# Four q/k buffers, eight first slots turned on TensorE, one assignment product per column set, and a new written-out order

## The chip, the cores and the metric

The kernel runs on one core of a Trainium2 chip. The core has a matrix engine (TensorE, "PE", whose weight loads are listed apart as "PEld"), VectorE ("DVE"), ScalarE ("ACT"), GpSimd ("POOL") and a sync engine ("SP") that issues nearly all transfers; 16 DMA engines carry them. Each engine works through its own list of instructions in order, and engines wait for each other by semaphores. The metric is the time of one execution on the device, in microseconds (us).

## The reference

Two layers follow each other. The first is attention inside clusters: queries and keys are each assigned to the nearest of 16 centroids, and a query attends only to keys of its own cluster. The second is a feed-forward network with a three-tap convolution along the sequence.

```python
# attention: q, k, v are [4, 8, 768, 64]; centroids [8, 16, 64]
q_assign = argmax(einsum(q_n, c_n)); k_assign = argmax(einsum(k_n, c_n))   # unit vectors
mask   = q_assign[:, :, :, None] == k_assign[:, :, None, :]
scores = where(mask, q @ k.T / 8, -1e9)
x      = softmax(scores) @ v                     # to [4, 768, 512]
# feed-forward: w_in [512, 1024], conv_w [3, 1024], w_out [1024, 512]
h    = relu(x @ w_in)
gate = sigmoid(conv3(h))
out  = (h * gate) @ w_out                        # float32 [4, 768, 512]
```

## The kernel before, in words

**Pairs and slots.** Two heads of one batch make a pair g, 16 in all (four per batch). A slot t is one pair against a part of its queries: 512 queries (the first part, `a` = 0) or 256 (`a` = 1). Of the eight slots of a batch the first four are its pairs with 512 queries, the next four the same pairs with 256. So slots 0 to 3 and 4 to 7 are batch 0, and 24 to 27 and 28 to 31 are batch 3. Scores are made with the keys on the partitions. One exponential step `E` works on 1024 columns; a slot has six of them in the first part and three in the second, 144 in all.

**The mask as extra rows.** The cluster of a query and of a key becomes three numbers (`BR`), which are appended to the 64 rows of q and k. The score product then has 67 rows and gives a large negative number wherever clusters differ, so that no mask step is needed.

**The way of a pair.** `LQ`, `LK` (pairs 0 to 7) or eight block loads `LZ` (pairs 8 to 15) bring q and k into a `qk_in` buffer, of which there are `NQK` in turn. `T` turns them on TensorE (line 295) and `Q` evicts the result, or `Z` turns blocks of 32 by 32 on VectorE (line 304). `A` multiplies them with the centroids (line 337), each of four 32-column sets of the array giving the similarities of a quarter of the tokens. `M0` to `M6` find the largest on VectorE; `M5` and `M6`, which pack the result, can be on GpSimd (`M5p`, `M6p`). `K` turns the pack on TensorE, `B` evicts it, and the transfer `BX` lays it as bias rows under q and k. `CC` casts q and k to half width, and the transfer `CX` shifts the second head to the lower partitions. `LV` loads v and `CV` casts it. In the first pair, one head at a time, `CD`, `KB` and `BB` do the work of `CC`, `K` and `B`.

**The way of a slot.** `S` is the score product, `E` the exponential on ScalarE (line 454), `V` the product with v (line 467), `P` the reciprocal of the row sums, `N` the normalization (line 490). The result has to be turned before it can enter the feed-forward part. There are two ways for it: `XD`, a transposing transfer on the sync engine's queue (line 508), or `X`, a transpose on TensorE (line 496), with `Ya` or `Yd`, an eviction on ScalarE or VectorE (line 308 or 310).

**The feed-forward part** goes in 24 units, six per batch: four units on the first 512 tokens, two on the other 256. `I` multiplies with w_in (line 534) and `R` evicts with the ReLU. `C` carries columns from one part to the next, on GpSimd. `a`, `b`, `c` are the taps on VectorE (lines 572 and 574), or `W` the taps on TensorE (line 580) with diagonal weights that `_tp` has made. `H` is the tanh on ScalarE, `G` the gate on VectorE (line 605), `O` the product with w_out (line 617, two of its eight terms a step), `F` its eviction into one of four `o_sb` buffers, `FX` the store. `LW` and `CW` load and cast the weights.

**What sets the order.** Nothing is scheduled at run time: `PLAN` is a list of some 1600 of these tokens, and the program issues them one after the other. So it lays down the order on every engine and on the sync engine's queue, on which all loads, stores, `CX`, `BX` and `XD` stand in one line. A token's `@n` names its bank of PSUM. The letter after a name, as in `Qa` or `Qd`, names the engine: a for ScalarE, d for VectorE, p for GpSimd.

```python
    for token in PLAN.split():
        step(token)
```

Of the kernel before, what the change touches and what calls it, by code (L numbers as in the profile page):

```python
# [15 lines left out]
NQK = 3  # L16
# [6 lines left out]
NBH = 1  # L23
# [138 lines left out]
def kernel(  # L162
# [92 lines left out]
    def heads(h):  # L255
        return slice(0, 2) if h is None else slice(h, h + 1)
# [624 lines left out]
```

## Time and profile before

| | us |
|---|---|
| three runs | 250.26, 253.67, 1277.74 |
| their median | 253.67 |
| the profiled execution | 249.97 |
| its span on the core | 247.8 |
| PE busy | 229.4 |
| VectorE busy | 212.1 |
| ScalarE busy | 210.1 |
| GpSimd busy | 77.8 |

The span runs from the first to the last instruction of the core; the time of the execution also holds what lies around it. A busy time counts an instruction from its start to its end, so that overlapping matmuls make PE look fuller than its work. In rows of waits, `A <- B: 2.4, 2, 1.9` says that A stood idle for 2.4 us until B was done, twice, 1.9 us the longer time. In groups of instructions the columns are line, engine, operation, tiles, shapes, count, then total us and mean ns, then the idle time before them. The chain of waits follows the instruction that ended last back to what released it, step by step.

### The profile page before, as it was taken

To read this page: it belongs to the slowest core of one execution; us is meant where nothing else is said; L and a number is where in the kernel's file an instruction comes from. 1 tells how busy PE (TensorE), PEld (TensorE's weight loads), DVE (VectorE), ACT (ScalarE), POOL (GpSimd) and SP (SyncE) were. 2 spreads that over 40 slices of the span, in tenths; PEclk is the share of its full clock that TensorE was granted. 3 is DMA by queue.
4 is the path that set the end of the run, shared out by engine and by line. 5 is a ranking of instruction groups with operands and counts; after the bars stand their busy time and mean duration, and the time that the engine had idled before them with its cause. 6 is when DMAs were issued, how large, how long until landed. Compare 5 with 4: busy or idle time off the path is not lost.

```text
span 247.8 us, 6354 instructions
## 1 busy us (share of the span) xinstructions
PE 229.4 (93%) x2443; PEld 146.2 (59%) x2443; DVE 212.1 (86%) x484; ACT 210.1 (85%) x277; POOL 77.8 (31%) x135
## 2 busy tenths in 40 slices
PE   8698889999898699969998999999999999999994
PEld 4465556557554466745465648764657677564661
DVE  4888775899999889976999999999999997899640
ACT  5586889998998699986998999998999999974442
POOL 3312352524265100462212011540365000449600
PEclk9999999999999999997999999999999999999999
DMA  6998979998779999999987961421207022111223
GB/s 147 269 247 136 221 236 289 374 264 139 140 156 164 125 131 159 118 210 197 138 161 170 172 193 55 99 57 32 70 15 224 3 66 65 42 45 54 107 96 127
DMA packets 97254, 35.40 MB, mean 143 GB/s; under 512 B 87537, under 2 KB 91657, under 8 KB 97225
## 3 DMA queue, kind: packets, MB, share of 16 engines
q1 hardware_dynamic: 97081, 34.97, 65.1%
q8 instruction: 19, 0.31, 0.6%
q14 instruction: 10, 0.08, 0.1%
q10 hardware_dynamic: 144, 0.03, 0.1%
HBM read 23.11 MB, written 6.29 MB: 119 GB/s over the span
## 4 chain that ended last, share of the span: by engine, by line
PE 38%; DVE 23%; ACT 16%; DMA 15%; issue 4%; SPq 3%; DVEq 0%; ACTq 0%
ACT attn L454 10%; DVE cnv L574 9%; PE flex L534 9%; PE sc L440 8%; PE flex L617 7%; DMA qk_in<-in_k_dram 5%; PE sc L617 4%; PE flex L467 4%; DMA xT<-x 3%; DVE hg L605 3%; DMA ext<-spk 3%; DMA ext<-ext 2%; DMA qk_in<-in_q_dram 2%; DVE x L490 2%; PE flex L295 2%
## 5 line engine op out<-in xcount | busy, mean ns | idle before, releaser
L454 ACT ACTIVATE attn<-sc 128x1024 f16<-128x1024 f32 x144 | 141.6, 1039 | 8.0 <-PE sc L440 7.6
L440 PE MATMUL sc<-ext 67*128 67x256 f16 (+1 forms) x384 | 83.9, 328 | 2.8 <-DMA ext<-spk 1.5
L574 DVE SCALAR_TENSOR_TENSOR cnv<-hpad,cwcol,cnv 128x510 f16<-128x510 f16 (+1 forms) x108 | 68.9, 658 | 0.5
L467 PEld LDWEIGHTS <-attn 128*128 128x128 f16 x1152 | 46.3, 97 | 14.5 <-ACT attn L454 2.9
L534 PE MATMUL flex<-xT,w_in 128*128 128x512 f16 (+1 forms) x248 | 48.7, 332 | 3.8 <-DMA xT<-x 2.4
L467 PE MATMUL flex<-v,attn 128*128 128x65 f16 x1152 | 50.5, 193 | 0.2
L440 PEld LDWEIGHTS <-ext 67*128 67x128 f16 x384 | 37.4, 113 | 21.9 <-issue 6.3
L310 POOL CAST ext<-qkT 128x768 f16<-128x768 f32 (+1 forms) x31 | 29.2, 960 | 52.9 <-PE sc L440 30.1
L617 PE MATMUL flex<-w_out,hg 128*128 128x512 f16 x144 | 38.7, 378 | 0.0
L534 PEld LDWEIGHTS <-w_in 128*128 128x128 f16 x256 | 24.7, 98 | 21.2 <-issue 6.4
L605 DVE SCALAR_TENSOR_TENSOR hg<-th,hpad 128x1020 f16<-128x1020 f32 (+3 forms) x31 | 30.4, 997 | 1.2 <-ACT th L597 1.2
L617 PEld LDWEIGHTS <-hg 128*128 128x128 f16 x192 | 17.7, 97 | 17.3 <-issue 0.6
L548 ACT ACTIVATE hpad<-flex 128x512 f16<-128x512 f32 x39 | 23.1, 608 | 5.3 <-PE flex L534 4.6
L597 ACT ACTIVATE th<-cnv 128x1020 f32<-128x1020 f16 (+1 forms) x21 | 22.5, 1073 | 3.0 <-DVE cnv L574 2.7
L557 POOL COPY hf<-hpad 128x6 f16<-128x6 f16 x16 | 5.7, 360 | 56.6 <-ACT hpad L548 51.7
L750 POOL TENSOR_SCALAR taps<-id,cwcol 128x128 f16<-128x128 f16 x24 | 21.2, 899 | 0.0
L490 DVE TENSOR_TENSOR x<-flex,rec 128x256 f16<-128x256 f32 x48 | 19.7, 415 | 0.5
L310 POOL CAST v<-v_in 128x768 f16<-128x768 f32 x13 | 12.4, 955 | 22.2 <-DMA v_in<-in_v_dram 14.1
L304 DVE STREAM_TRANSPOSE qkT<-qk_in 128x384 f32<-128x384 f32 x32 | 16.8, 552 | 2.5 <-DMA qk_in<-in_k_dram 2.2
L572 DVE TENSOR_SCALAR cnv<-hpad,cwcol 128x510 f16<-128x510 f16 (+1 forms) x54 | 17.4, 344 | 1.7 <-ACT hpad L548 1.5
L295 PE MATMUL flex<-id,qk_in 128*128 128x128 f32 x96 | 14.9, 281 | 2.4 <-ACT qkT L308 0.7
L337 PE MATMUL flex<-qkT,cP 128*32 128x192 f32 x240 | 12.9, 332 | 1.9 <-DVE x L490 1.2
(86 smaller groups left out, 190.1 us busy)
## 6 DMA issues: line engine op xcount, KB each, us to landing
v_in<-in_v_dram SPq DMA_DIRECT2D x16, 384.0 KB
out_dram<-o_sb SPq DMA_DIRECT2D x24, 256.0 KB
qk_in<-in_q_dram SPq DMA_DIRECT2D x16, 192.0 KB
qk_in<-in_k_dram SPq DMA_DIRECT2D x16, 192.0 KB
qk_in<-in_q_dram SPq DMA_DIRECT2D x32, 96.0 KB
qk_in<-in_k_dram SPq DMA_DIRECT2D x32, 96.0 KB
ext<-ext SPq DMA_DIRECT2D x15, 192.0 KB
hg<-in_moe_w_in_dram SPq DMA_DIRECT2D x4, 512.0 KB
```

The costliest lines, as they stand in the source:

```text
L310: (nc.vector if name == "d" else nc.gpsimd).tensor_copy(out=to, in_=src)
L440: nc.tensor.matmul(to[:, m], lhsT=keys[:, kt], rhs=ext_b[g % NE][0:KR, h, 0, Q0[a] : Q0[a] + QN[a]], start=True, stop=True, skip_group_che ...
L454: nc.scalar.activation(to, sc[at].rearrange("p n s -> p (n s)"), AF.Exp, scale=0.125)
L467: nc.tensor.matmul(avp(at)[:, jq + (2 * h if a else 0), 0 : D + 1], lhsT=attn[t, i // 3][:, o : o + P], rhs=v16_b[g % NE][:, h, kt, 0 : D ...
L490: nc.vector.tensor_tensor(out=to, in0=src, in1=by, op=ALU.mult)
L534: nc.tensor.matmul(bank[at][:, QN[a] * f : QN[a] * (f + 1)], lhsT=w_in16[:, r, f0 + (a + 1) * p + f, :], rhs=xT[:, b % 2, r, Q0[a] : Q0[a] ...
L548: nc.scalar.activation(to, src, AF.Relu)
L574: nc.vector.scalar_tensor_tensor(out=cnv, in0=src, scalar=w, in1=cnv, op0=ALU.mult, op1=ALU.add)
L597: nc.scalar.activation(to, pre, AF.Tanh, scale=0.5)
L605: nc.vector.scalar_tensor_tensor(out=hg_b[b][:, f0 + fs.start : f0 + fs.stop, LO[a] : LO[a] + N], in0=rows_of(th_t[n], n)[:, fs], scalar=1 ...
L617: nc.tensor.matmul(bank[at][:, 0:Dm], lhsT=hg_b[b][:, fb, P * tq : P * (tq + 1)], rhs=w_out16[:, fb, :], start=(fb == 0), stop=(fb == NFB ...
L750: nc.gpsimd.tensor_scalar(out=taps16[:, fb, kk, :], in0=id16[:], scalar1=cwcol[:, fb, kk : kk + 1], scalar2=None, op0=ALU.mult)
```

## The change

Four things are changed.

1. `NQK` is 4 instead of 3: a fourth `qk_in` buffer.
2. `assign` makes one product for q and k together. For each of the four column sets it issued two matmuls of 192 columns, one for q and one for k; it now issues one of 384. (`turn_rows` now reads the pack through `pack_of`; it reads the same elements.)
3. The output of slots 4 to 7 is turned on TensorE (`X`) instead of by a transfer (`XD`), so that with 0 to 3 the first eight slots go that way. For slots 28 and 29 it is the other way round: `XD` in place of `X`. There were 24 `XD` and 8 `X`; there are 22 and 10.
4. `PLAN` is laid out anew. The tokens are the same kinds and, but for the ones above, the same number; their order, their banks and for some their engine differ.

```diff
-NQK = 3
+NQK = 4
...
     def assign(g, h, at):
         sims_at[g, h] = at
         b, h0 = batch_pair(g)
-        for x in range(2)[heads(h)]:
-            tokens = qkT[g][:, x].rearrange("p (c j t) -> p j c t", c=J, j=4)
-            w = cH[:, x] if g < NBH else cP[:, g % NPR]
-            o = 0 if h is not None else 192 * x
-            for j in range(4):
-                nc.tensor.matmul(
-                    bank[at][32 * j : 32 * (j + 1), o : o + 192],
-                    lhsT=w,
-                    rhs=tokens[:, j],
...
+        if h is None:
+            tokens, w, o = qkT[g].rearrange("p x (c j t) -> p j x c t", c=J, j=4), cP[:, g % NPR], 2 * 192
+        else:
+            tokens, w, o = qkT[g][:, h].rearrange("p (c j t) -> p j c t", c=J, j=4), cH[:, h], 192
+        for j in range(4):
+            nc.tensor.matmul(
+                bank[at][32 * j : 32 * (j + 1), 0:o],
+                lhsT=w,
+                rhs=tokens[:, j],
...
     def turn_rows(g, h, x, at):
 
         turn_at[g, h, x] = at
-        pack = pack_tile(g, h)[:, 0 : 6 * J].rearrange("p (r i) -> p i r", r=BR)
+        pack = pack_of(g, h if g < NBH else None)[:, :, h if g >= NBH else 0, x]
         for j in range(J):
-            nc.tensor.transpose(bank16[at][D:KR, P * j : P * (j + 1)], pack[:, J * x + j], id16[:])
+            nc.tensor.transpose(bank16[at][D:KR, P * j : P * (j + 1)], pack[:, :, j], id16[:])
```

Of `PLAN`, the stretch around slots 7 and 8:

```diff
-    "E.7.0@1 V.6.2@1 LZ.8.1.2 S.7.1@0 M2.6 LZ.8.0.2 Ra.3.0 S.7.2@1 P.6.0 CCp.6.1 Rd.3.1 E.7.1@0 LZ.9.0.0 "
-    "O.0.0.0@2 c.3.0 LZ.9.1.0 T.7.0@0 N.6.0 E.7.2@1 c.3.1 S.8.0@0 LZ.9.0.1 M3.6 T.7.1@1 a.3.0 LZ.8.1.3 Qa.7.0 "
-    "S.8.1@1 C.3 M4.6 Qa.7.1 BX.5 C.1 T.7.2@0 c.1.1 "
-    "E.8.0@0 V.7.0@1 N.5.0 LZ.8.1.0 V.7.1@1 a.1.1 V.7.2@1 E.8.1@1 O.0.1.0@3 XD.6 P.7.0 CCp.7.0 Z.8.0 S.8.2@0 "
...
+    "E.7.0@1 b.0.1 LZ.8.1.3 X.5@3 T.6.1@1 V.6.2@2 C.4 Yd.5 BX.4 H.0 a.1.1 S.7.2@1 T.6.2@3 CVp.4 P.6.0 Qd.6.1 "
+    "LV.5 E.7.1@0 LZ.8.0.2 N.6.0 T.7.0@1 a.1.0 Qa.6.2 X.6@2 Ya.6 b.1.1 A.6@3 Qa.7.0 CX.5 E.7.2@1 b.1.0 "
+    "T.7.1@2 LZ.8.1.0 T.7.2@1 CCp.6.1 M0.6 Qa.7.1 M1.6 V.7.0@3 Qa.7.2 CCp.6.0 LZ.8.0.3 X.4@2 V.7.1@3 H.1 Yd.4 "
+    "V.7.2@3 A.7@1 G.0 LZ.8.0.1 S.8.0@0 LV.6 S.8.1@1 M2.6 "
```

What the new order does elsewhere, counted in tokens: before the first exponential of slot 12 (`E.12.0`) stood 109 transfer issues, now 100; before `E.16.0` 132, now 116. `M5` is on GpSimd for eleven pairs instead of six, `M6` for six in both. Seven pairs (2, 3, 4, 5, 10, 14 and 15) now have `M5` on GpSimd and `M6` on VectorE, before only pair 9. Q/k evictions (`Q`) are 16 on ScalarE and 9 on VectorE, before 14 and 11.

More of the change, by code (lines that the diff above doesn't have):

```diff
@@ L331, in assign @@
         b, h0 = batch_pair(g)
-        for x in range(2)[heads(h)]:
-            tokens = qkT[g][:, x].rearrange("p (c j t) -> p j c t", c=J, j=4)
-            w = cH[:, x] if g < NBH else cP[:, g % NPR]
-            o = 0 if h is not None else 192 * x
-            for j in range(4):
-                nc.tensor.matmul(
-                    bank[at][32 * j : 32 * (j + 1), o : o + 192],
-                    lhsT=w,
-                    rhs=tokens[:, j],
-                    start=True,
-                    stop=True,
-                    skip_group_check=True,
-                )
+        if h is None:
[7 more added lines that the diff above has]
+                rhs=tokens[:, j],
+                start=True,
+                stop=True,
+                skip_group_check=True,
+            )
     def pack_tile(g, h):
```

253 rows, old and new, of the table PLAN are left out of this document.

## The prediction

> **What bounds the kernel now.** I read the page's busy times, then the transfers by slice, then busy times by stretch, then who waited for whom, and last the sync engine's own order. Busy times first (engine, us, share of the span, instructions):
>
> ```profile
> PE 229.4 (93%) x2443; PEld 146.2 (59%) x2443; DVE 212.1 (86%) x484; ACT 210.1 (85%) x277; POOL 77.8 (31%) x135
> ```
>
> No engine alone is the bound: three lie within 20 us of each other. Where they idle shows in the transfers, 40 slices of 6.2 us in tenths:
>
> ```profile
> DMA  6998979998779999999987961421207022111223
> ```
>
> The 16 DMA engines are near full for 24 slices (149 us), mostly idle after. The same cut as busy time by stretch (length; busy us and instructions of each engine; granted clock; DMA share; GB/s):
>
> ```profile
> 13.74:140.00 126.26, 115.67 (x1360) 74.61 (x1359) 110.86 (x253) 112.85 (x143) 38.82 (x55) 0.99 0.96 187
> 140.00:200.00 60.00, 59.28 (x662) 38.32 (x660) 59.25 (x139) 57.55 (x74) 18.49 (x27) 1.00 0.33 88
> 216.50:244.95 28.45, 27.81 (x204) 16.35 (x202) 18.83 (x34) 15.91 (x29) 12.88 (x18) 1.00 0.23 84
> ```
>
> 13.74 is the first exponential, 216.5 the first of the last slot. At DMA share 0.33 PE idles 0.72 of 60 us; at 0.96 it idles 126.26 - 115.67 = 10.59, VectorE 15.40 and ScalarE 13.41. The first 140 us are slowed by transfers, the next 76 are full, and the last 28 belong to PE. What PE itself waited for on transfers between 13.74 and 140 (us, times, longest), and VectorE below it:
>
> ```profile
> PE flex L534 <- DMA xT<-x: 2.4, 2, 1.9
> PE sc L440 <- DMA ext<-spk: 1.5, 2, 0.9
> ...
> PE flex L295 <- DMA qk_in<-in_k_dram: 0.7, 1, 0.7
> ...
> PE flex L295 <- DMA qk_in<-in_q_dram: 0.2, 1, 0.2
> ```
>
> ```profile
> DVE qkT L304 <- DMA qk_in<-in_k_dram: 2.2, 3, 1.8
> ```
>
> Why they are late: the sync engine issues nearly everything, one after another (start, length):
>
> ```profile
> 68.28 0.83 SPq L407 DMA_DIRECT2D ext<-spk  x1
> 69.15 0.44 SPq L280 DMA_DIRECT2D qk_in<-in_k_dram  x1
> 69.70 1.20 SPq L508 DMA_TRANSPOSE xT<-x  x1
> 71.00 0.55 SPq L324 DMA_DIRECT2D ext<-ext  x1
> ```
>
> There is hardly a gap between them (0.1 us). A transposing transfer (XD, line 508) holds the queue longer than a block load (LZ, line 280); min/median/max ns:
>
> ```profile
> L508 SPq DMA_TRANSPOSE xT<-x x24: 1168/1222/2215, 63.4 to 203.6; - x24
> ```
>
> ```profile
> L280 SPq DMA_DIRECT2D qk_in<-in_q_dram x32: 428/524/2661, 54.0 to 138.2; - x32
> ```
>
> And it empties the DMA engines around itself: their share from 68 to 72 us, a tenth of a us per digit.
>
> ```profile
> DMA  9999889999999997433220059999669961000000
> ```
>
> From about 69.6 the share falls to nothing, the transfer runs for about 1.2 us, and nothing follows for 0.6.
>
> **The change, part by part.** The sum is against the profiled execution: 249.97 us, 247.8 of it span. The three runs shown are 250.26, 253.67 (the median) and 1277.74, so the profiled one stands 0.1% under the lowest and 1.5% under the median.
>
> *Transfers taken out early, and set further ahead.* XD of slots 4 to 7 goes; those of 28 and 29 come back at the end. Up to E.12.0 the plan had 109 issues, 6 of them XD; now 100, 2 of them XD. Up to E.16.0 it is 132 against 116, with 12 block loads fewer. Four XD are 4 x 1.2 us of the queue and four drains. Distances, counted in exponentials from the last block load to the VectorE turn that needs it: the shortest was 2 (pair 9) and is now 3. From the last XD of a group to the first product that reads it the shortest was 2 (slots 12-15), now 3. One exponential:
>
> ```profile
> 93.90 6.72 ACT L454 ACTIVATE attn<-sc 128x1024 f16<-128x1024 f32 x7
> ```
>
> that is 0.96 us each. Transfers on the chain of waits (start, length):
>
> ```profile
> 15.56 6.03 DMA ext<-ext
> ...
> 29.63 2.83 DMA ext<-spk
> ...
> 69.70 2.35 DMA xT<-x
> ...
> 80.94 3.51 DMA ext<-spk
> ...
> 106.46 5.06 DMA xT<-x
> ```
>
> So 3 exponentials (2.9 us) hide an XD on a free queue (2.35), not one behind others (5.06). Bias rows (BX) have not moved ahead: three or fewer exponentials lie between BX and its scores for 7 of 15 pairs before and 7 after. Hence I take PE's waits for xT and q/k (2.4 + 0.7 + 0.2 = 3.3) as gone, those for bias rows (1.5) as staying, half of VectorE's 2.2 as gone, and 0.6 for waits that carry another engine's name but go back to a late transfer: 3.3 + 1.1 + 0.6 = **-5.0**. Ends: nothing, if the next wait in line is as long; and 10.59 less the idle share of the later stretch (126.26 x 0.72 / 60 = 1.5), **-9.1**.
>
> *The fourth q/k buffer.* Its direct worth is what loads waited for a buffer, in the sync engine's waits of the first 140 us:
>
> ```profile
> SPq L270 <- PE sc L440: 1.4, 3, 0.6
> ...
> SPq L270 <- PE flex L295: 1.0, 1, 1.0
> ...
> SPq L270 <- PE flex L337: 0.3, 1, 0.3
> ```
>
> 2.7 us of queue at most, hidden unless the load is late; it is inside the term above.
>
> *One product per column set.* A float32 matmul leaves two records, so a pair's sixteen records of 192 columns become eight of 384. PE, in order of time:
>
> ```profile
> 6.82 0.53 PE L337 MATMUL flex<-qkT,cH 128*32 128x192 f32 x8 [0.41 <-ACT qkT L308]
> ...
> 14.12 0.86 PE L337 MATMUL flex<-qkT,cP 128*32 128x192 f32 x16
> ...
> 26.00 0.40 PE L496 MATMUL flex<-id,x 128*128 128x128 f16 x4
> 26.24 0.60 PE L440 MATMUL sc<-ext 67*128 67x512 f16 x2
> ...
> 45.54 0.60 PE L440 MATMUL sc<-ext 67*128 67x256 f16 x4
> ```
>
> If instructions count, a pair costs 0.53 and saves 0.33; if columns do, it saves nothing: 15 pairs, 0 to -5.0. The last two rows decide: four of 256 columns take as long as two of 512, so columns count. I take 0.05 a pair, of which two thirds fall where PE ends the path: **-0.5**. The Trainium skill (TensorEngine Tiling (Array Packing), Instruction Overhead) gives every matmul about 60 cycles on top; at the 2.4 GHz of its page TensorE: Matmul & The Clock Gate that is an estimate of 25 ns, 0.2 us for eight, 3 us in all, and the sum would end 2.5 lower. The two score rows speak against it.
>
> *Turns on PE.* Slots 4 to 7 add eight transposes, 28 and 29 take four away; four start 0.24 apart from the next (26.00 to 26.24), so +0.24 on PE. Evictions, beside two prices that the reshuffle needs:
>
> ```profile
> L310 DVE COPY qkT<-flex 128x512 f32<-128x512 f32 x10 | 6.7, 684 | 0.4 <-PE flex L399 0.2
> L308 ACT ACTIVATE qkT<-flex 128x512 f32<-128x512 f32 x11 | 6.4, 618 | 3.1 <-PE flex L295 3.1
> ...
> L308 ACT ACTIVATE xT<-flex 128x256 f16<-128x256 f16 x3 | 1.2, 391 | 0.9 <-PE flex L496 0.9
> ...
> L310 DVE COPY xT<-flex 128x256 f16<-128x256 f16 x1 | 0.3, 280 | 0.0
> ```
>
> Two more on VectorE (0.28 each) and two more short ones on ScalarE (0.39) against two fewer elsewhere. On three nearly full engines that is **+0.4**; between 0 and +1.0.
>
> *Engines reassigned.* On VectorE six long steps (two of them q/k evictions, 0.68 each) go and four come, and five pack steps go to GpSimd:
>
> ```profile
> L310 POOL CAST ext<-qkT 128x768 f16<-128x768 f32 x29 | 26.9, 945 | 46.4 <-PE sc L440 30.1 <-DVE qkT L310 8.1 <-DVE qkT L304 5.2
> ...
> L386 POOL TENSOR_SCALAR pack<-best 128x24 f16<-128x24 f32 x6 | 1.5, 249 | 9.9 <-DVE best L379 6.7 <-DVE rec L478 3.2
> L386 DVE TENSOR_SCALAR pack<-best 128x24 f16<-128x24 f32 x9 | 1.4, 155 | 0.2
> ```
>
> 2 x 0.68 + 5 x 0.155 = 2.1 less for VectorE; ScalarE comes out even. But a wait is added: for seven pairs, not one, step M5 is now on GpSimd and M6 on VectorE, which stands still with the tap products and normalizations behind it until GpSimd is done: 7 x 0.25 = 1.7, and up to 7 x 0.95 more if a cast is ahead on GpSimd. Cover is that GpSimd is 31% busy. Net 2.1 - 1.7, not always on the path: **0**, between -2.1 and +6. Two more q/k evictions (0.62) stand on ScalarE before the first exponential; they come out of the next stage, so nothing, or +1.2 if nothing is gained there.
>
> *The end.* XD of 28 and 29 take four transposes off PE, where PE bounds. Nine output steps of two 512-column matmuls lie between XD.29 and the first product that reads it, against 2.35 us of landing: hidden; the price if not is 2.35. Behind XD.28 on the queue stand stores that nobody waits for there. Zero.
>
> Sum: -5.0 - 0.5 + 0.4 + 0 = -5.1, and 249.97 - 5.1 = **244.9 us**, 2.0% less.
>
> **The rivals.** *A, the engines fill first.* From 140 to 200 us three engines are 96 to 99% busy, and no work leaves them; then only direct PE waits on xT count, 2.4, with +0.4 and the ScalarE start +1.2 against it: 249. For it: ScalarE's largest waits are for PE, not transfers. Against it: 10.59 us of PE idle.
>
> *B, bias rows come late (slower).* BX waits for the shift of its pair to land, and the scores wait for BX. Distances BX to scores, pair 1 to 15, were 1 3 4 6 6 2 3 4 6 3 6 5 2 3 6 and are 0 4 3 2 4 2 5 3 3 5 7 3 4 4 5 exponentials. At 3.51 us a landing the uncovered parts add up to 8.3 before and 9.2 after; at 6.03, the length of a shift under load, to 33 and 39. That is +6.5: with no relief elsewhere 256.5 us. It decides once landings stay near 6 us. Against it: the queue is shorter where they are issued.
>
> *C, an XD is no dearer than another transfer.* Then taking four out relieves nothing, xT's 2.4 stays and the drain gap is chance: 244.9 + 2.4 = 247. For it: only one stretch was looked at closely. The Trainium skill says so (Advanced Engine Details and Errata, X-Bar Transpose): such transfers are as fast as regular ones. The two issue rows, 1222 against 524 ns, disagree at the queue.
>
> *D, the buffer is not used:* the new order issues loads later, not sooner, so three buffers would do. It changes no time: 244.9.
>
> **How the numbers follow.** A measurement here tells about 2% from no change, 5 us. Forecast (with D) 0.52, of it 0.39 beyond 2% and 0.13 within, since it lies on the bound and its first term has more room below than above; A 0.24, of it 0.02 beyond; C 0.09, within; B 0.15, of it 0.12 slower by over 2% and 0.03 within. Faster 0.41, same 0.47, slower 0.12. The likeliest case alone runs from 240.5 to 247.5. The range adds A and C and the lower part of B: 240.5 to 252.5; it leaves out most of B and the far end of the first term.
>
> **What would show it.** Right: DMA share below 0.9 and PE idle below 7 us between the first exponential and the one that stood at 140; no wait of PE on xT above 0.5; sync engine gaps before 120 us. The product: a pair near 0.8 us. Wrong: waits on ext<-spk over 4 us (B), or ScalarE and VectorE idle as before with short transfers (A).

## The result, and the profile after

| | before | after |
|---|---|---|
| median of the first runs, us | 253.44 | 241.47 |
| ratio, 95% interval | | 0.956 [0.944, 0.967] |
| median when run again, beside more runs of before | 250.59 | 241.35 |
| ratio, 95% interval | | 0.967 [0.962, 0.971] |
| the profiled execution | 249.97 | 241.51 |
| its span | 247.8 | 239.3 |

The changed kernel is faster by 3.3 to 4.4%. The ratios here and below are made from the runs within 1.5% of a kernel's fastest, so that they can differ from the quotient of two medians, and the profiled executions of experiments 5 and 6 lie above that. The profiled execution was forecast to fall by 5.1 us, to 244.9; it fell by 8.5, to 241.51, which lies inside the range of 240.5 to 252.5. The page of the changed kernel, in three views (busy times, transfers by slice, the shares of the chain of waits by engine):

```profile
PE 226.0 (94%) x2327; PEld 142.9 (60%) x2327; DVE 208.7 (87%) x481; ACT 208.8 (87%) x277; POOL 78.2 (33%) x140
...
DMA  6996899999998779974985999480121204003123
...
PE 55%; DVE 25%; DMA 7%; ACT 6%; issue 3%; SPq 1%; POOL 1%; DVEq 0%; ACTq 0%
```

In the kernel before, the shares of the chain were:

```profile
PE 38%; DVE 23%; ACT 16%; DMA 15%; issue 4%; SPq 3%; DVEq 0%; ACTq 0%
```

They show what kind of program it has become: PE now carries 55% of the chain, before 38%, and transfers 7%, before 15%. Gaps have appeared in the transfers: a 4 at 108 to 114 us and a 5 at 126 to 132, where before no digit under 7 stood between 6 and 142 us.

The same cut by stretch as for the kernel before (length; busy us and instructions of PE, PE's weight loads, VectorE, ScalarE, GpSimd; granted clock of PE; DMA share; GB/s):

```profile
13.74:140.00 126.26, 119.86 (x1333) 75.47 (x1328) 116.15 (x269) 117.56 (x152) 40.84 (x62) 1.00 0.91 184
140.00:200.00 60.00, 59.28 (x643) 39.13 (x642) 58.42 (x138) 58.00 (x73) 17.77 (x25) 1.00 0.44 102
```

In the first stretch PE idles 6.4 us where it idled 10.6, and VectorE and ScalarE idle some 5 us less. The clearer cut is by the work: from the first exponential to that of slot 18, from there to slot 31, and the rest. First the kernel before, then the changed one:

```profile
13.74:136.30 122.56, 111.97 (x1301) 71.48 (x1300) 107.65 (x246) 109.19 (x138) 38.82 (x55) 0.99 0.95 188
136.30:216.50 80.20, 79.48 (x874) 52.56 (x872) 76.65 (x176) 77.61 (x99) 21.45 (x32) 1.00 0.33 85
216.50:247.80 31.30, 27.81 (x204) 16.35 (x202) 18.83 (x34) 15.91 (x29) 12.88 (x18) 1.00 0.23 85
```

```profile
12.47:130.20 117.73, 111.32 (x1227) 68.85 (x1226) 108.20 (x244) 108.79 (x140) 37.62 (x58) 1.00 0.91 183
130.20:210.20 80.00, 79.28 (x844) 52.79 (x842) 76.81 (x180) 77.06 (x98) 23.71 (x37) 1.00 0.47 108
210.20:239.30 29.10, 25.43 (x197) 15.34 (x193) 15.20 (x28) 14.31 (x27) 14.10 (x17) 1.00 0.23 84
```

So the 8.5 us are 1.3 up to the first exponential, 4.8 from there to slot 18, 0.2 in the full stretch, and 2.2 at the end, where PE has 27.81 - 25.43 = 2.4 us less to do. That work was done earlier: behind the first exponential of slot 31 the new list has two `I`, one `O` and one `V` fewer and one `W` more, and ahead of that of slot 18 four `O` more. The 4.8 of the second part are 4.2 us less idle time of PE (10.59 to 6.41) and 0.65 less busy time.

From the waits of the changed kernel in its first 132 us: those of PE and its weight loads on transfers, and, first, one that is new:

```profile
DVE pack L394 <- POOL pack L386: 0.4, 1, 0.4
PEld L440 <- DMA ext<-spk: 0.4, 1, 0.4
PEld flex L294 <- DMA qk_in<-in_k_dram: 0.3, 1, 0.3
PE sc L440 <- DMA ext<-spk: 0.2, 1, 0.2
```

Before, PE stood 4.8 us for transfers (2.4 + 1.5 + 0.7 + 0.2) and VectorE 2.2 in its q/k turns. Now it is 0.2 and, in this time, nothing; one such wait of VectorE is left, behind the start of slot 18:

```profile
DVE qkT L303 <- DMA qk_in<-in_q_dram: 0.6, 1, 0.6
```

### The profile page after: what moved, and what is told of

The parts are those of the page before. It is cut to its first block, busy times and chain, and to the rows that moved or that the text cites. A ratio compares the mean times of both kernels' runs of the same rounds, so it can differ in the third digit from the quotient of the medians.

```text
span 239.3 us, 6107 instructions
## 1 busy us (share of the span) xinstructions
PE 226.0 (94%) x2327; PEld 142.9 (60%) x2327; DVE 208.7 (87%) x481; ACT 208.8 (87%) x277; POOL 78.2 (33%) x140
## 4 chain that ended last, share of the span: by engine, by line
PE 55%; DVE 25%; DMA 7%; ACT 6%; issue 3%; SPq 1%; POOL 1%; DVEq 0%; ACTq 0%
PE sc L440 14%; PE flex L617 12%; PE flex L534 10%; PE flex L467 8%; DVE cnv L574 7%; PE flex L337 4%; DMA qk_in<-in_q_dram 3%; ACT attn L454 3%; DVE qkT L303 2%; PE sc L617 2%; DVE sim L363 2%; DMA qk_in<-in_k_dram 2%; DVE eqq L372 2%; DVE cnv L572 2%; PE flex L681 2%
## 5 line engine op out<-in xcount | busy, mean ns | idle before, releaser
L574 DVE SCALAR_TENSOR_TENSOR cnv<-hpad,cwcol,cnv 128x510 f16<-128x510 f16 (+1 forms) x108 | 67.5, 655 | 0.1
L467 PEld LDWEIGHTS <-attn 128*128 128x128 f16 x1152 | 47.6, 97 | 16.2 <-issue 2.5
L534 PE MATMUL flex<-xT,w_in 128*128 128x512 f16 (+1 forms) x240 | 46.4, 329 | 0.8 <-DVE hpad L550 0.5
L617 PE MATMUL flex<-w_out,hg 128*128 128x512 f16 x168 | 44.9, 379 | 0.9 <-DVE x L490 0.4
L309 POOL CAST ext<-qkT 128x768 f16<-128x768 f32 (+1 forms) x28 | 25.6, 936 | 45.3 <-PE sc L440 32.1
L548 ACT ACTIVATE hpad<-flex 128x512 f16<-128x512 f32 x40 | 24.0, 616 | 2.3 <-PE flex L534 1.9
L750 POOL TENSOR_SCALAR taps<-id,cwcol 128x128 f16<-128x128 f16 x24 | 21.5, 910 | 0.0
L294 PE MATMUL flex<-id,qk_in 128*128 128x128 f32 x96 | 14.0, 279 | 0.7 <-ACT qkT L307 0.3
L337 PE MATMUL flex<-qkT,cP 128*32 128x384 f32 x120 | 13.0, 498 | 0.9 <-ACT qkT L307 0.7
L309 POOL CAST v<-v_in 128x768 f16<-128x768 f32 x14 | 11.7, 836 | 5.9 <-DMA v_in<-in_v_dram 3.0
```

What stands on the lines that cost most here:

```text
L309: (nc.vector if name == "d" else nc.gpsimd).tensor_copy(out=to, in_=src)
L337: nc.tensor.matmul(bank[at][32 * j : 32 * (j + 1), 0:o], lhsT=w, rhs=tokens[:, j], start=True, stop=True, skip_group_check=True,)
L467: nc.tensor.matmul(avp(at)[:, jq + (2 * h if a else 0), 0 : D + 1], lhsT=attn[t, i // 3][:, o : o + P], rhs=v16_b[g % NE][:, h, kt, 0 : D ...
L534: nc.tensor.matmul(bank[at][:, QN[a] * f : QN[a] * (f + 1)], lhsT=w_in16[:, r, f0 + (a + 1) * p + f, :], rhs=xT[:, b % 2, r, Q0[a] : Q0[a] ...
L548: nc.scalar.activation(to, src, AF.Relu)
L574: nc.vector.scalar_tensor_tensor(out=cnv, in0=src, scalar=w, in1=cnv, op0=ALU.mult, op1=ALU.add)
```

## The experiments

The median of each is compared with runs of the kernel before on the same chip (251.07, 251.13 and 250.59 in three groups). The lines of a program shift with its edits and with the lines in which its list is set, so that the line numbers can be lower by 1, 13 or 14 than in the kernel before. Two tables ahead, so that each experiment can be read against the others. First the two halves of the change, its list and its parts (the buffer, the turns of slots 4 to 7, the product; slots 28 and 29 go with the list), as ratios to the kernel before:

| | old list | new list |
|---|---|---|
| old parts | 1 | 1.011 [1.006, 1.015] |
| new parts | 1.000 [0.997, 1.004] | 0.967 [0.962, 0.971] |

Second, where in the profiled execution of each the time lies. The start of a slot is that of its first exponential:

| kernel | start of slot 4 | of slot 9 | of slot 18 | 18 to 31 | from 31 to the end |
|---|---|---|---|---|---|
| before | 46.2 | 75.3 | 136.3 | 80.2 | 31.3 |
| after | 45.2 | 74.3 | 130.2 | 80.0 | 29.1 |
| new list, three buffers | 46.1 | 78.0 | 135.8 | 79.7 | 29.0 |
| new list, two products | 45.8 | 76.5 | 132.9 | 80.0 | 29.1 |
| new list, slots 4 to 7 by transfer | 44.7 | 78.8 | 134.2 | 80.3 | 29.1 |
| the same, its wait filled | 45.8 | 79.7 | 133.8 | 80.3 | 29.0 |
| new list, none of the parts | 45.0 | 84.3 | 140.9 | 79.8 | 29.1 |
| old list, four buffers | 48.7 | 77.8 | 140.3 | 80.4 | 31.3 |
| old list, slots 4 to 7 on TensorE | 48.9 | 78.9 | 139.2 | 80.1 | 31.6 |
| old list, all parts | 47.8 | 77.9 | 137.6 | 80.1 | 31.6 |

The last column goes by the list alone, and the one before it hardly moves. All else is decided before slot 18, and the differences between the columns tell where. From slot 9 to slot 18 the new list takes 54 to 58 us whatever parts it has, and the old one 60 to 63. From slot 4 to slot 9 the old list takes 29 to 30 us with its parts or without; the new one takes 29.1 with all of them, 31.9 with three buffers, 34.1 with slots 4 to 7 by transfer and 39.3 with none. So in these executions, one of each kernel, the list wins its time behind slot 9 and at the end, and the parts save what it would otherwise lose ahead of slot 9.

**1. The new list with three buffers.**

```diff
-NQK = 4
+NQK = 3
```

> The changed kernel with NQK = 3 and nothing else undone. Theory (late transfers were the cost, and the new order relieves them): the new order issues loads later than the old one, so three buffers do almost as well: 241.5 to 242.5 us against 241.5. Rival (the fourth buffer carries the gain): the sync engine stands still for buffers that are not free, waits of loads on TensorE and VectorE grow beyond 5 us in the first 140 us, and the time is 245 or more.

Measured: 246.99 us, ratio 0.982 [0.978, 0.987]. Taking the buffer away costs 5.6 us of the gain. The sync engine's waits for this kernel, and then PE's:

```profile
SPq L279 <- PE flex L294: 5.4, 1, 5.4
SPq L279 <- DVE qkT L303: 3.5, 1, 3.5
```

```profile
PE flex L294 <- DMA qk_in<-in_k_dram: 1.8, 1, 1.8
```

The new list puts the first load of pair 9 (`LZ.9.0.0`) ahead of the turn of pair 6 (`T.6.0`). With three buffers pair 9 takes the buffer of pair 6, so the whole queue stands for 5.4 us until that pair is turned, and the load of pair 7's k behind it comes 1.8 us late for PE. A later load stands 3.5 us for a buffer that VectorE has not turned yet, and from 66.6 to 69.8 us the granted clock is 0.50, behind the 1.8 us of PE's wait. With four buffers, pair 9 takes that of pair 5. The buffer is used, and my own theory, that it is not, falls.

**2. The new list with two products.** The old `assign` in the changed kernel.

> The changed kernel with two 192-column products per column set again. Theory: columns count, not instructions; a pair takes 0.86 us instead of about 0.82, so 241.5 to 242.3. Rival (each matmul has a fixed cost): eight instructions a pair cost 0.2 to 0.33 us, 3 to 5 in all: 244.5 to 246.5.

Measured: 244.58 us, ratio 0.968 [0.958, 0.977]. The median is that of the rival, but the ratio is nearly that of the changed kernel (0.967), and the rows show that two products cost next to nothing more than one. A pair of the changed kernel, and of this one, each with the step that follows it:

```profile
76.22 0.85 PE L337 MATMUL flex<-qkT,cP 128*32 128x384 f32 x8
77.01 0.61 PE L440 MATMUL sc<-ext 67*128 67x512 f16 x2
```

```profile
78.43 0.86 PE L336 MATMUL flex<-qkT,cP 128*32 128x192 f32 x16
79.22 0.60 PE L439 MATMUL sc<-ext 67*128 67x512 f16 x2
```

Both hold PE for 0.79 us from start to start. Elsewhere it is 0.78 against 0.79, so 15 pairs save at most some 0.15 us. The rest of the 3.2 us between the medians has another place. PE's rows of this kernel near the start of slot 4, and then its stretches (the granted clock is the third number from the end):

```profile
44.80 0.23 PE L398 MATMUL flex<-id,pack 128*128 128x128 f16 x1 [0.94 <-DVE pack L393]
...
46.89 1.00 PE L439 MATMUL sc<-ext 67*128 67x256 f16 x4 [0.48 <-ACT attn L453]
```

```profile
47.00:49.00 2.00, 2.00 (x19) 1.63 (x18) 1.12 (x2) 1.77 (x2) 2.00 (x3) 0.50 1.33 249
49.00:51.00 2.00, 2.00 (x9) 0.95 (x8) 0.00 (x0) 1.09 (x2) 1.34 (x2) 0.66 0.83 186
```

The changed kernel waits there too, 0.43 and 0.48 us, and keeps its clock at 1.00. Here it is 0.94 and 0.48, and for some 3.4 us the clock is half. A single run of this kernel with a mean clock of 0.998 took 241.88, half a us more than the changed kernel. Why the wait for the pack is 0.94 and not 0.43, the runs don't say.

**3. The new list with slots 4 to 7 by transfer.** `X.4` to `X.7` become `XD.4` to `XD.7` where they stand; `Ya` and `Yd` of these slots go.

> The changed kernel with slots 4 to 7 turned by transposing transfers again, issued where the TensorE transposes stood; 28 and 29 stay transfers. Theory: four transfers of 1.2 us on the queue and four drains of the DMA engines delay what is behind them, 2 to 3 us come through: 243.5 to 244.5, with waits of PE on xT again. Rival (such a transfer is no dearer than another and there is room): 241 to 242, if anything faster by the 0.4 us that the turns cost on the engines.

Measured: 247.06 us, ratio 0.982 [0.976, 0.987]: 5.7 us of the gain, twice what the theory said. In the profiled execution, 245.75 us, it is one wait of PE before slot 9, and a lowered clock behind it (rows of the waits, then stretches):

```profile
PE flex L521 <- DMA xT<-x: 3.6, 1, 3.6
```

```profile
71.00:73.00 2.00, 0.00 (x0) 0.00 (x0) 1.83 (x4) 0.00 (x0) 1.42 (x2) 1.00 0.56 110
73.00:75.00 2.00, 1.96 (x10) 1.04 (x10) 0.00 (x0) 1.21 (x2) 0.95 (x2) 0.74 1.01 164
75.00:77.00 2.00, 2.00 (x16) 1.51 (x15) 0.00 (x0) 1.27 (x2) 0.00 (x0) 0.50 1.19 170
```

**4. The new list alone**, with three buffers, two products and slots 4 to 7 by transfer.

> The new order alone: three buffers, two products, slots 4 to 7 by transfer, all in the new list. Theory: the distances of the loads in the new list keep more than half of the gain, about 5 of 9 us: 244 to 246. Rival (the parts carry it and the list only fits them): 249 or more, as before the change.

Measured: 253.85 us, ratio 1.011 [1.006, 1.015]. The theory falls: the list without its parts keeps none of the gain and is slower than the old one. PE's wait for xT is longer than ever, and VectorE waits for q:

```profile
PE flex L520 <- DMA xT<-x: 5.8, 2, 4.0
DVE qkT L290 <- DMA qk_in<-in_q_dram: 5.6, 2, 5.2
```

**5. The old list with four buffers.** `NQK = 4` in the kernel before.

> The kernel before with one edit: four q/k buffers instead of three; its list is untouched. Theory (the parts are worth something only with a list that issues loads for them; the old list was written for three buffers, so that its loads wait 2.7 us for a buffer in all): the time stays within 1.5 us of the kernel before, 249.5 to 252.5, and PE's waits on xT (2.4) stay as they are. Rival (the buffer by itself carries what its removal from the new list cost, about 5 us): 247.5 or less.

Measured: 251.9 us, ratio 1.001 [0.997, 1.005]. The theory holds in the time: the old list gains nothing from the buffer. PE's waits on xT did not stay at 2.4 us; in the profiled execution, 254.24 us, they are longer:

```profile
PE flex L534 <- DMA xT<-x: 3.6, 3, 1.6
```

**6. The old list with slots 4 to 7 on TensorE.** For each of them, `XD.t` becomes `X.t` and an eviction, in its place or right behind its normalization.

> The kernel before with one edit: slots 4 to 7 are turned on TensorE in place of the four transposing transfers, each at the place that its transfer had or right behind its normalization. Theory (parts and list only work together): the four transfers leave the queue, but the loads behind them are not needed sooner by anything that bounds; 249.5 to 252.5. Rival (each transposing transfer costs its queue time and a drain wherever it stands, 4 x (1.2 + 0.6) = 7.2 us of queue, of which at least a third reaches PE): 248.5 or less, with slot 9 starting 2 us sooner than in the kernel before.

Measured: 250.85 us, ratio 0.992 [0.988, 0.996]. The median lies within the theory's range, the ratio (0.8% under the kernel before) between the two expectations, and slot 9 does not start sooner (this execution came 2.7 us late to slot 4, with a lowered clock at 40 us). From slot 4 to slot 17 this execution takes 78.0 us and that of the kernel before 81.0, so 3.0 us are won, some 1.7 of them because the lowered clock that the kernel before has at 111 us is missing here; but slot 17 then lasts 12.3 us and not 9.1. The gain is given back at the next wait. Experiments 7 and 9 show the same: their slot 17 lasts 12.4 and 11.2 us. The sync engine's last transposing transfer before slot 18, in the kernel before and in this one, and PE's wait for it:

```profile
130.03 1.36 SPq L508 DMA_TRANSPOSE xT<-x  x1
```

```profile
130.85 1.17 SPq L494 DMA_TRANSPOSE xT<-x  x1
...
135.17 0.71 PE L520 MATMUL flex<-xT,w_in 128*128 128x256 f16 x5 [2.60 <-DMA xT<-x]
```

The engines come sooner, the transfer does not: the queue is full between 112 and 130 us in both. In the changed kernel it is issued 3.2 us sooner:

```profile
126.83 1.20 SPq L508 DMA_TRANSPOSE xT<-x  x1
```

**7. The old list with plain copies for slots 4 to 7.**

```diff
-             transpose=True,
+             **({} if t in (4, 5, 6, 7) else {"transpose": True}),
```

> The kernel before with one edit: the transfers of slots 4 to 7 move the same bytes without transposing them, so that these columns of xT are not turned and the output differs. Theory (the transposing form itself is dear): the queue is held 0.5 to 0.7 us by each instead of 1.2, the share of the DMA engines does not fall to nothing around it, and the time comes out like that of the kernel with the turns on TensorE, within 1 us. Rival C (a transposing transfer is no dearer than another): the same hold, the same landing, and 250.5 to 252.5.

Measured: 249.63 us, ratio 0.995 [0.991, 0.999], not to be told from experiment 6. The hold of the queue, min/median/max in ns, came out as the theory said, 516 against 1222:

```profile
L508 SPq DMA_DIRECT2D xT<-x x4: 473/516/542, 64.2 to 77.3; - x4
```

The share of the DMA engines did so only in part. From 68 to 72 us, a tenth of a us per digit, first this kernel, then that of experiment 6, which has no such transfer at all here:

```profile
DMA  9999999999999998212211048999879610099898
```

```profile
DMA  9999999720122101599999979594999077869999
```

The hole of 0.7 us before the middle, which I had put down to the transposing transfer, is there in all three kernels, so that transfer does not make it. In each it begins some 1.3 us after the bias rows' transfer was issued (at 68.28, 68.31 and 67.58 us); why, the runs do not say. The second hole, at 71.4 us in the kernel before, does shrink: from 0.7 us to 0.3 with plain copies, while the queue is held 0.7 us less.

**8. The kernel of experiment 3 with its wait filled.** In front of the matmul of unit 5 that waits for xT, 34 matmuls add zeros to its bank.

```diff
+FILL = {(5, 1, 0, 3): 34}
...
             for r in range(R):
+                for _ in range(FILL.get((n, p, f, r), 0)):
+                    nc.tensor.matmul(bank[at][:, 0:256], lhsT=zero[:, 0:P], rhs=zero[:, 0:256], start=False, stop=False, skip_group_check=True)
                 nc.tensor.matmul(
```

> The changed kernel with slots 4 to 7 turned by transfers (247.06 us in an earlier run), and 34 matmuls of 256 columns with zero weights put in front of the matmul of unit 5 that waited 3.6 us for xT there; they add zeros to the same bank. The transfer lands when it landed before. Theory (a granted clock of 0.50 for some 3.4 us follows when PE has stood idle, at a price of about 1.7 us): no clock below 0.9 behind this wait, slot 9 starts about 1.7 us sooner than 78.8, and 245.0 to 246.0. Rival (the lower clock has another cause, such as the burst of work after the wait): it comes all the same, 246.5 to 248.

Measured: 244.16 us, ratio 0.970 [0.965, 0.975], which is 2.9 less than without the filling and more than the theory said. The transfer came no sooner (PE went on at 75.6 us, with slot 8 at 68.8; without the filling at 73.0, with slot 8 at 66.1). The clock stayed up behind the wait (this execution has a lowered clock elsewhere, at 47 us):

```profile
73.00:75.00 2.00, 2.00 (x21) 1.79 (x19) 2.00 (x5) 0.00 (x0) 1.08 (x2) 1.00 0.85 216
75.00:77.00 2.00, 2.00 (x17) 1.39 (x16) 0.17 (x1) 0.67 (x2) 1.29 (x2) 1.00 1.10 165
77.00:79.00 2.00, 2.00 (x22) 1.42 (x21) 0.68 (x4) 2.00 (x3) 0.00 (x0) 1.00 1.12 166
```

From slot 8 to slot 10 it takes 19.7 us and not 21.5: 1.8 for the lowered clock, as expected. So a wait that PE fills does not lower the clock, and the lowered clock costs time of its own, on top of the wait. The other 1.1 us of the median are not accounted for by one profile of each.

**9. The old list with all the parts**: buffer, turns of slots 4 to 7, product.

> The kernel before with all the parts and none of the list: four q/k buffers, slots 4 to 7 turned on TensorE, one assignment product per column set; the old list otherwise. Theory (parts and list work only together; with the turns alone the 3 us won by slot 17 went into a wait of 2.6 us for the transposing transfer before slot 18, because all that stands ahead of it on the queue still does): 249 to 251, PE waits for xT near 132 to 136 us for over 1.5, a ratio of 0.99 to 1.0 to the kernel before. Rival (the three parts add up by themselves and the list only rearranges): 247 or less.

Measured: 250.34 us, ratio 1.000 [0.997, 1.004]. The theory holds, the wait before slot 18 with it:

```profile
133.94 0.71 PE L521 MATMUL flex<-xT,w_in 128*128 128x256 f16 x5 [1.61 <-DMA xT<-x]
```

**10. The kernel before with its wait filled**, by 17 such matmuls ahead of the one of unit 7 that waits at 109.6 us.

> The kernel before with 17 matmuls of 256 columns with zero weights ahead of the matmul of unit 7 that waits 1.9 us for xT at 109.6 us, adding zeros to its bank. The transfer lands when it did. Theory (a clock of 0.50 for 3.6 us behind this wait costs about 1.7 us in the runs that have it): a profile without a clock under 0.9 at 111 to 115 us, and 249.0 to 250.0. Rival (the time lost there is made up by the next wait for a transfer): the clock stays up and the time stays, 250.5 to 251.5.

Measured: 252.51 us, ratio 1.008 [1.003, 1.013]. The theory's first half holds, its time falls. First the kernel before, then this one:

```profile
111.00:113.00 2.00, 1.44 (x5) 0.71 (x5) 2.00 (x7) 0.39 (x1) 0.28 (x1) 0.56 0.96 141
113.00:115.00 2.00, 2.00 (x9) 0.96 (x7) 2.00 (x5) 1.23 (x2) 0.00 (x0) 0.59 0.94 287
```

```profile
111.00:113.00 2.00, 2.00 (x14) 1.20 (x13) 2.00 (x7) 1.42 (x2) 0.00 (x0) 1.00 0.82 152
113.00:115.00 2.00, 2.00 (x28) 1.45 (x27) 1.78 (x3) 1.78 (x4) 1.86 (x2) 1.00 1.06 290
...
132.00:134.00 2.00, 0.20 (x2) 0.14 (x2) 2.00 (x3) 0.00 (x0) 0.00 (x0) 0.69 0.37 88
134.00:136.00 2.00, 2.00 (x9) 1.14 (x8) 0.72 (x1) 0.68 (x2) 0.72 (x1) 0.50 0.76 187
```

Slot 17 starts 2.1 us sooner (125.2 against 127.3), and then PE waits 3.1 us for the same transfer as in experiment 6, and the clock falls there instead. The rival (made up by the next wait) is right on the mechanism; the time is even a little worse than it said.

**11. The changed kernel again.** No edit.

> The changed kernel once more, unedited, to have it beside the others. Theory and rival agree: 241 to 242, a ratio of 0.958 to 0.966 to the kernel before.

Measured: 241.35 us, ratio 0.967 [0.962, 0.971]: the time as said, the gain 0.1 percentage points short of it.

**12. The changed kernel with M5 on VectorE** for the seven pairs that have it on GpSimd and M6 on VectorE (`M5p.2` becomes `M5.2`, and so on).

> The changed kernel with step M5 of pairs 2, 3, 4, 5, 10, 14 and 15 on VectorE as M6 is, so that VectorE has 7 x 0.155 = 1.1 us more and no wait for GpSimd between the two. Theory (the wait showed as 0.4 us in one place, where PE then stood 0.43 us before turning the pack of pair 5): the time of the changed kernel within 0.6 us, and less idle time of PE at 44 us, so that runs with a lowered clock there are rarer. Rival (the wait costs what the prediction bounded it by, 1.7 us or more): 240 or less.

Measured: 241.34 us, ratio 0.967 [0.963, 0.971]: the theory holds, the added wait costs nothing that can be measured. PE's wait of 0.43 us before the turn of pair 5's pack is gone. Whether lowered clocks are rarer, six runs cannot tell.

## Why the prediction was right, and where it was not

*What bounds the kernel* was right: transfers in the first 140 us, three full engines to 216, PE at the end. The middle stretch kept its 80 us in all ten kernels of the second table, whatever was done before it, and PE's direct waits on transfers went.

*Transfers taken out early, and set further ahead* (-5.0). The size is near: the stretch to which it belongs gave 4.8. In part that is luck. Its direct PE waits on xT and q/k (3.3) went, as said. Two of its parts were mis-sized: the bias-row waits, which I let stand at 1.5, fell to 0.2, and VectorE's 2.2, of which I took half, to 0.6. PE's direct waits alone fell by 4.6, and its idle time in that stretch by 4.2, so nothing shows the 1.1 and the 0.6 that I added for VectorE and for waits under another name. And the reason given for the term failed. I argued from distances in the list and from four transfers fewer, each worth its own queue time. Distances alone (experiment 4) lose 1.1%, and the parts alone (experiment 9) give nothing. Together they give 3.3%. The gain belongs to the two jointly: the list wins behind slot 9, and only with the parts does it not lose more than that ahead of slot 9.

*The fourth q/k buffer*, put inside that term at no more than 2.7 us of queue, and rival D (the buffer is not used, three would do): this step failed. I took its worth from what loads waited for a buffer in the old list, but the new list is written for it. In the new list its removal costs 5.6 us; in the old its addition gives nothing. The new list does show it: `LZ.9.0.0` stands ahead of `T.6.0`, and with three buffers the load cannot go until the turn is done; in the old list it stands behind it.

*Rival C* (an XD is no dearer than another transfer) is wrong in its time, and the row stands: 1222 ns of queue against 516 for the same bytes untransposed. The Trainium skill (Advanced Engine Details and Errata, X-Bar Transpose) has transposing transfers as fast as regular ones; experiment 7 does not bear that out for the issue, and no row here tells the landing of the two. My other ground against C, that such a transfer empties the DMA engines around itself, failed for the first hole, which is there without it, and held for the second.

*One product per column set* (-0.5): the direction was right, that columns count and not instructions, but 0.05 a pair was too much. It measures 0.01 at most, 0.15 us in all. The 3 us of the Trainium skill's rule (TensorEngine Tiling (Array Packing), Instruction Overhead) are nowhere in it. The two thirds by which I multiplied came from no row.

*Turns on PE* (+0.4) and *engines reassigned* (0): no run singles out the first, and nothing in the runs speaks against either. The wait from GpSimd to VectorE showed once, 0.4 us, not seven times 0.25, and experiment 12 puts the whole at nothing.

*The end* (0) failed: it gave 2.2 us. I looked only at the turns and at whether `XD.28` and `XD.29` are covered. The new list does 2.4 us more of PE's work before slot 31, and the middle stretch, full as it was, grew no longer. The fourth experiment has the same 29.1 us, so that the list alone brings this, with none of the parts.

*What was not in the sum*: the first exponential is 1.3 us sooner, all of it taken back within slot 0 (slot 1 starts at 24.9 and 24.8), and the kernel before had some 3.4 us of half clock behind its xT wait at 111 us. The clock stood in its windows as 0.99 for the whole stretch, and I passed over that. A steadier clock does not explain the gain: of the 61 runs of the kernel before that stand beside the experiments, the 12 with a mean granted clock of 0.996 or more have a median of 250.1 us, and all 61 one of 251.0; the changed kernel has 241.35.

*Rivals A and B* fell. ScalarE and VectorE did not hold PE back (its idle time fell by 4.2), and bias rows are waited for 0.2 us. Of *what would show it*, PE's idle time below 7 us (6.4) and no wait on xT came true; the DMA share came to 0.91 where I said below 0.9. The pair near 0.8 us tells nothing, since it was as near before. The sync engine has gaps between 35 and 120 us, where the kernel before has none of over 0.7 us, such as the one from 73.84 to 76.87. That sign is weak too, since a gap can be a wait of the next transfer in line: the slower kernel of experiment 4 has one of 7.5 us.

```profile
71.26 2.58 SPq L284 DMA_DIRECT2D v_in<-in_v_dram  x2
76.87 0.77 SPq L407 DMA_DIRECT2D ext<-spk  x1
```

## What to carry to other kernels

Where a queue bounds a stage, engine time that is won ahead of the queue's last transfer comes back as a wait for that transfer: look for the step at which the queue is caught up with, and move that. A resource is worth what the order that uses it needs, so price a buffer in the new list (which load would stand behind which release), not by the waits of the old one, and measure parts and order in a square of four. And a wait of PE can be dearer than its length, since a lowered clock can follow it; filling the wait pays (experiment 8) unless the next wait takes the time back (experiment 10).

## What the runs showed of the hardware

PE's granted clock fell to 0.50 after short idle times, for 3.4 to 3.6 us in nine places of the profiles (their last few us left out), read in stretches of 0.2 us; in two more it was renewed, to 7.0 and 10.4 us. It followed in each case on 1.2 to 2.6 us of idle time of PE within the 3.4 us before, not always in one piece: the 1.9 us wait in the kernel before, 0.94 and 0.48 in experiment 2. It did not follow each such stretch: the kernel before had 2.0 us of idle time from 81.0 to 84.4 us without it, and experiment 4 had 2.2 from 61.3 to 64.7. The changed kernel had 0.9 us where experiment 2 had its 1.4, and kept its clock. At half clock PE does 1.7 to 1.8 us less work in that time, and experiment 8 measured 1.8. What it costs depends on the next wait: the 61 runs of the kernel before have medians of 250.1 us at a mean granted clock of 0.996 and more, 250.3 near 0.993, 251.2 near 0.986 and 252.4 below 0.983. So runs of one kernel differ by a few us according to how often the clock falls, and three or four of them are few.

The Trainium skill (TensorE: Matmul & The Clock Gate, HAM oscillation — how this bites in real kernels) has the clock fall after gaps of over 3.4 us. In experiment 3 it fell after a wait of 3.6 us, which agrees; in experiment 4 it fell 1.6 us into a wait of 4.0, and in the other nine places the gaps were shorter, such as the 1.9 us of the kernel before. Matmuls with zero weights on zeros, which do no work, kept the clock up (experiment 8).
